# One store ahead of two transposing transfers, two memsets behind a copy: a segment-recurrent attention block with a gated MLP, forward and backward

## The chip, the core and the metric

The kernel runs on one NeuronCore of one Trainium2 chip. A core has TensorE (PE, matrix products into PSUM), VectorE (DVE), ScalarE (ACT), GpSimd (POOL) and SyncE (SP), which here only issues DMA transfers. Each engine works through its own instructions in order and waits on semaphores for the others. The metric is the device time of one execution in microseconds; lower is better. Times of a kernel are the median of several runs. A profile comes from one execution, which has a time of its own.

## The reference

The forward pass, and then the gradients of its result with respect to ten inputs for a given `grad_out`. Inputs are bf16; there are 2048 rows of width 512.

```python
def attention(x, mem):                    # 64 segments of 32 rows, 8 memory rows, 32 heads of 128
    for s in range(64):
        h = concat([mem, x[32*s : 32*s + 32]])           # 40 rows
        q, k, v = h @ Wq, h @ Wk, h @ Wv                 # per head
        p = softmax(where(mask, q @ k.T * 128**-0.5, -1e9))
        o = (p @ v) @ Wo
        mem = o[:8]                                      # goes to the next segment
        yield o[8:]
def mlp(x):                               # hidden width 1792
    return (sigmoid(x @ w_gate) * (x @ w_up)) @ w_down
sa, ca, ga, sb, cb, gb = split(silu(c) @ w_mod, 6)
x = x + ga * attention(layernorm(x) * (1 + ca) + sa, mem0)
x = x + gb * mlp(layernorm(x) * (1 + cb) + sb)
out, vjp = jax.vjp(all_of_the_above);  return out, *vjp(grad_out)
```

The memory rows make the forward pass a recurrence over 64 segments, and the backward pass one in the other direction.

## The kernel before

The kernel has four long stages, one after the other.

- **Forward recurrence** (`phase2`, a loop over s = 0 to 63). A segment projects K, Q and V (`proj`, `v_chunk`), turns them on PE (`turns`), computes the transposed scores and their exponentials (`st_exp`, ACT, into ET), the sums (`den`, `recip`), P V (`pv`), scales it into Ost (`ost`), turns it (`ott_first`, `ott_rest`, into OT), multiplies by Wo (`outproj`) and hands the memory rows on. For the backward pass it stores, by SP, V transposed (VT), P (PS), O (OSR) and O transposed (OT), each a tensor of 128 x 11 x 128 bf16 per segment, and the rows of K and Q (KST, QST).
- **GLU** (`phase3`, the gated MLP, forward and backward, 16 tiles of 128 rows). Its steps s0 to s6 are run as a pipeline, the deepest step first. Behind it come the products for the weight gradients of the MLP, between which the attention weights are loaded and turned.
- **Backward recurrence** (`phase4`, s = 63 to 0).
- **Weight gradients of the attention** (`phase5`).

The order is written out by hand. `pin` ties the instructions of a stretch on one engine to each other in the order of the program; `pin_behind` ties instructions of an engine behind the last one of an earlier stretch. An instruction that is tied by neither goes where its own inputs and buffers let a scheduler put it.

**Around the first edit.** P is made of ET by a transposing SP transfer into Pst (L1065), which the step `norm` (L1157) multiplies on POOL by the reciprocal sums (L1158). Its store to PS is kept in the list `stores_p` (L1161). `norm` of segment s is run in segment s + 1, ahead of the projections (L988), or in segment 63 behind Q's and K's first half there (L1002). The store is issued later in that segment, behind the transposing transfers of V (L1057, into the one buffer VTr) and P (L1065) of the segment itself (L1066). Pst has two buffers, used in turn; the second is `self.Pst1`.

SP's order in segment 62 (NS - 2) is therefore: KST and QST of the segment (L609, L610), L1057, L1065, the store of P of segment 61 ("the last but two"), OSR (L1094), OT (L1133).

In segment 63 the first tile of the GLU is prepared beside the attention (`first_tile_steps`): `add` makes x1 = a * ga + x0 (L770, L771), `stats` (L774 to L777) and `scale` (L780) its normalisation. x1 lies in `first_x1`, which is a view of `self.Pst1`: the buffer of the odd segments, 61 among them. `add` (`first_tile[3]`, L990) stands ahead of K's and Q's projections of segment 63 on DVE, so that DVE's casts of their results (RA1k, RA1q, line L63, in the helper `evac`) come behind it. PE's transposes of RA1k are line L893.

Also in segment 63, POOL issues the loads of the GLU's weights: w_gate and w_up into the place of Wk (L1000, L1001) as soon as K's products are done, w_down into that of Wv (L1044) behind V's. In the GLU, PE reads w_gate from L1341 on, w_up from L1345 on, and w_down in the transposes of L1250.

**Around the second edit.** The last tile's last steps in the GLU: s5 makes hp on PE (L1412); ACT copies it (dh2b, L1418); DVE makes dxh (L1421), pr_cb, junk, bb, cc, ta; ACT tb (L1437); DVE dx (L1439), da, pr_ga; then s6 on PE sums rows into `acc_ps` (L1455) and turns da (L1459). At the end DVE copies `acc_ps` out (L1541, `accs`). Two memsets that belong to the backward recurrence are written further down: of `dOst` (L1602), rows of dO, whose tails are first filled in the third chunk of the last weight gradient of the GLU, and of the first 8 columns of `dyT` (L1861). Nothing ties them, and in the kernel before they stand among the last tile's steps on DVE: the first ahead of dxh, the second between ta and dx.

Of the kernel before, what the change touches and what calls it, by code (L numbers as in the profile page):

```python
# [40 lines left out]
class K:  # L41
# [407 lines left out]
    def phase2(self):  # L449
        nc, tc, cfg, io = self.nc, self.tc, self.cfg, self.io  # L450
        D, DC, H, E, L, M, T, G, NS = cfg.D, cfg.DC, cfg.H, cfg.E, cfg.L, cfg.M, cfg.T, cfg.G, cfg.NS
# [14 lines left out]
        with ExitStack() as ctx:  # L466
# [10 lines left out]
            def ps_f32(name):  # L477
                return psp.tile([128, PG, GW], F32, name=name, tag="p")
# [328 lines left out]
            stores_p = []  # L807
# [34 lines left out]
            def tails_in(xs, s):  # L842
                for x in xs:
                    to_heads("pool", XT[x], btails[s // nseg_t][x][:], 0, 8, 8, 8 * (s % nseg_t))
# [15 lines left out]
            for s in range(NS):  # L860
# [13 lines left out]
                QT, KT, Vst, ET, OT = XT["q"], XT["k"], Vsts[s % 2], ETs[s % 2], OTs[s % 2]  # L874
# [176 lines left out]
                if 0 < s < NS - 1:  # L1051
                    v_chunk(s, 2)
                    v_tails(s + 1)
                    if s4 < 3:
                        tails_in("kq", s + 1)
                if s < NS - 1:
                    nc.sync.dma_start(VTr[:], Vst[:, :], transpose=True)  # L1057
                or2 = ps_f32("or_ps")
                den(0, or2)
# [142 lines left out]
    def phase3(self):  # L1202
# [9 lines left out]
        with ExitStack() as ctx:  # L1212
# [264 lines left out]
            def load_hr(g):  # L1477
                w, n = min(384, F - 384 * g), NT
                (nc.sync if g == 1 else nc.scalar).dma_start(
                    hrs[g][:, 0:n, 0:w], self.HHROWS[0:128 * n, 384 * g:384 * g + w].rearrange("(j p) f -> p j f", p=128))  # L1480
# [12 lines left out]
            def wd_chunk(fc, ps, ot):  # L1493
                if fc >= 3:
                    wd_products(fc, ps, range(NT))
                self.evac("act" if kk[0] % 2 == 0 else "dve", ot[:], ps[:])
                kk[0] += 1
                nc.gpsimd.dma_start(io["out_9"][fc * 128:(fc + 1) * 128, :], ot[:])
# [25 lines left out]
            ET = mybir.EngineType  # L1524
# [14 lines left out]
            self.pin_behind(i0, self.pinned, [ET.PE, ET.DVE, ET.Activation, ET.Pool, ET.SP])  # L1539
            accs = self.flat(self.Wk, 2 * DC * F, 2 * D, F32)  # L1540
            nc.vector.tensor_copy(accs[:], acc_ps[:, :])  # L1541
            for i in range(4):
                nc.gpsimd.dma_start(self.DMOD[2 + i:3 + i, :], accs[32 * i:32 * i + 1, :])

# [3 lines left out]
        with ExitStack() as ctx:  # L1548
            op_ = ctx.enter_context(tc.tile_pool(name="p3g_o", bufs=2, reuse_waits="tile"))
            psG = ctx.enter_context(tc.tile_pool(name="p3g_ps", bufs=4, space=PSUM, reuse_waits="tile"))  # L1550
            setup_pieces = self.p4_weights_setup_pieces(ctx)
            units = 3 * (FC - 3) + 8 * 2 * NCH * DC
            psE = ctx.enter_context(tc.tile_pool(name="p3g_pe", bufs=2, space=PSUM, reuse_waits="tile"))
            n_setup, done = len(setup_pieces), [0]

            def emit_setup(n):
                done[0] += n
                while setup_pieces and (n_setup - len(setup_pieces)) * units < done[0] * n_setup:
                    setup_pieces.pop(0)()
            i0 = len(self.traced())  # L1560
            h2r = self.flat(self.Wk, NT * D, NT * D).rearrange("p (j d) -> p j d", j=NT)
            load_hr(2)
            xrs = []

            def load_xr(i):
                if i < 2 * NCH:
                    rows, ch = ((self.DGROWS, self.DUROWS)[i // NCH], i % NCH)
                    t = ring[i % 2].rearrange("p (j f) -> p j f", j=NT)
                    nc.scalar.dma_start(t, rows[:, ch * CH:(ch + 1) * CH].rearrange("(j p) f -> p j f", p=128))
                    xrs.append(t)  # L1570

            for fc in range(3, FC):
                wd_chunk(fc, psG.tile([128, D], F32, name="gps2", tag="g"), op_.tile([128, D], BF16, name="ot2", tag="o"))
                if fc == 5:
                    load_hr(3)
                elif fc == 8:
                    load_hr(4)
                elif fc == 9:
                    nc.scalar.dma_start(h2r, self.H2ROWS[:, :].rearrange("(j p) d -> p j d", p=128))
                elif fc == 11:  # L1580
                    load_xr(0)
                emit_setup(3)
            load_xr(1)
            k = kk[0]
            for (rows, outw) in ((self.DGROWS, io["out_7"]), (self.DUROWS, io["out_8"])):
                for ch in range(NCH):
                    xr = xrs.pop(0)
                    for c in range(DC):
                        ps = psG.tile([128, CH], F32, name="gps", tag="g")
                        for j in range(NT):  # L1590
                            nc.tensor.matmul(ps[:], lhsT=h2r[:, j, c * 128:(c + 1) * 128], rhs=xr[:, j, :],  # L1591
                                             start=(j == 0), stop=(j == NT - 1))
                        ot = op_.tile([128, CH], BF16, name="ot", tag="o")
                        self.evac("act" if k % 2 == 0 else "dve", ot[:], ps[:])
                        k += 1
                        nc.gpsimd.dma_start(outw[c * 128:(c + 1) * 128, ch * CH:(ch + 1) * CH], ot[:])
                        if c == DC - 1:
                            load_xr(NCH * (outw is io["out_8"]) + ch + 2)
                        emit_setup(8)
                    if outw is io["out_7"] and ch == 0:  # L1600
                        self.get_db(cfg.NS // 4 - 1)
                        nc.vector.memset(self.dOst[:], 0.0)  # L1602
                    if outw is io["out_8"] and ch < 2:
                        self.first_dO_pass(psE, ch)
                    elif outw is io["out_8"] and ch == 2:
                        self.first_dO_turns(psE)
            while setup_pieces:
                setup_pieces.pop(0)()
            self.pin(i0, [mybir.EngineType.SP])
# [37 lines left out]
    def get_da(self, t):  # L1647
        if t not in self.das and t >= 0:
            d = self.dap.tile([128, 4, self.cfg.DC, self.cfg.T], BF16, name="daq")
            self.nc.sync.dma_start(d[:].rearrange("p s c t -> p s (c t)"),  # L1650
                                   self.DAOT[4 * t:4 * t + 4].rearrange("s p c t -> p s (c t)"))
            self.das[t] = d
        return self.das.get(t)
# [60 lines left out]
    def phase4(self):  # L1714
        nc, tc, cfg, io = self.nc, self.tc, self.cfg, self.io
        D, DC, H, E, L, M, T, G, NS = cfg.D, cfg.DC, cfg.H, cfg.E, cfg.L, cfg.M, cfg.T, cfg.G, cfg.NS
# [5 lines left out]
        with self.p4_ctx as ctx:  # L1722
# [52 lines left out]
            def get_dy(s):  # L1775
                if s not in dys:
                    t = dyp.tile([128, DC, 32], BF16, name="dyT")
                    nc.gpsimd.tensor_copy(t[:, :, M:32], get_da(s // 4)[:, s % 4, :, 0:32 - M])
                    dys[s] = t
                return dys[s]  # L1780
# [77 lines left out]
            nc.gpsimd.dma_start(self.DHA[NS, 0:M, :], dSs[0][0:M, 0:D])  # L1858
            self.pin(i0, [mybir.EngineType.Pool, mybir.EngineType.SP])
            dyT = get_dy(NS - 1)  # L1860
            nc.vector.memset(dyT[:, :, 0:M], 0.0)  # L1861
            nseg_t = 128 // T
            row_stores = []

# [664 lines left out]
```

## Time and profile before

| | |
|---|---|
| median of 3 runs | 2963.39 us (2962.72 to 2967.39) |
| the profiled execution, its own time | 2965.28 us |
| its span, first to last instruction | 2963.4 us |
| mean granted clock of PE | 0.998 |
| busy: PE / DVE / ACT / POOL | 98 / 55 / 45 / 42 % of the span |
| forward recurrence, segment 62 to 63 | about 14 us each, to 949 us |
| GLU's pipeline | about 949 to 1275 us |

Reading it: a time in a timeline counts from the start of the span. `[2.32 <-DMA PS<-Pst]` behind a row says that the engine stood idle for 2.32 us ahead of it and what came last of what it waited for. PE's matmuls overlap, so that a busy PE is not a PE at its peak. The granted clock is a share of PE's full clock. Names lose their buffer numbers: `Pst` is either buffer, and `Pst` written by L770 is x1. SPq is SP's DMA queue: a row gives the time of the issue, not that of the transfer. Line L63 is the DVE branch of a helper through which most copies go, L61 the ACT branch.

### The profile page before, as it was taken

How to read it: one execution, taken by the hardware profiler on the slowest of the kernel's cores; microseconds unless marked ns; L12 is line 12 of the kernel's file. 1: busy time of each engine (PE TensorE's matmuls, PEld its weight loads, DVE VectorE, ACT ScalarE, POOL GpSimd, SP SyncE). 2: the span in 40 equal slices, each digit the busy share in tenths (PEclk: the TensorE clock that was granted, in tenths of full speed). 3: DMA queues.
4: the chain of work that ended last, by engine and by line, in shares of the span. 5: the costliest groups of instructions: out<-in, count | busy, mean ns of one | idle time of the engine just before them, and what ended most of it. 6: DMA issues, size and time to landing. Idle time of an engine off the chain costs nothing.

```text
span 2963.4 us, 105252 instructions
## 1 busy us (share of the span) xinstructions
PE 2908.1 (98%) x43764; PEld 1815.4 (61%) x43838; DVE 1630.8 (55%) x3686; ACT 1343.5 (45%) x3245; POOL 1234.7 (42%) x2487
## 2 busy tenths in 40 slices
PE   7999999999998999999999999999999999999999
PEld 3666666666665544445677777777777754445545
DVE  5565666666556888733456666665666642750011
ACT  3666666666666433312355555554555520110011
POOL 2555555555554222221344444444444432762111
PEclk9999999999999999999999999999999999999999
DMA  9888888888889899998699999999999997886565
GB/s 311 230 222 217 227 220 216 222 228 213 217 232 270 216 233 229 242 289 269 189 252 252 253 248 253 258 248 244 253 256 252 250 282 242 255 260 190 164 215 170
DMA packets 838065, 703.00 MB, mean 237 GB/s; under 512 B 537698, under 2 KB 710162, under 8 KB 836692
## 3 DMA queue, kind: packets, MB, share of 16 engines
q1 hardware_dynamic: 711972, 485.29, 65.8%
q0 software_dynamic: 54512, 148.63, 15.5%
q10 hardware_dynamic: 71104, 62.34, 6.6%
q8 instruction: 345, 5.65, 0.8%
q14 instruction: 132, 1.08, 0.1%
HBM read 294.99 MB, written 276.35 MB: 193 GB/s over the span
## 4 chain that ended last, share of the span: by engine, by line
PE 64%; DMA 1%; DVE 1%; issue 1%; ACT 1%; SPq 0%; POOL 0%; DVEq 0%; POOLq 0%; ACTq 0%
PE gps L2308 14%; PE dh_ps L215 8%; PE g_ps L1931 5%; PE pass_ps L257 5%; PE gps5o L2323 4%; PE dhq_ps L223 4%; PE mm L1412 3%; PE gps L1591 3%; PE dh_tps L215 3%; PE mm L1387 2%; PE mm L1372 2%; PE tps L1848 2%; PE mm L1341 1%; PE mm L1345 1%; PE gps L1490 1%; PE turn_ps L1804 1%
## 5 line engine op out<-in xcount | busy, mean ns | idle before, releaser
L2308 PE MATMUL gps<-rows,hrows 128*128 128x512 bf16 (+2 forms) x2124 | 413.6, 355 | 1.9
L2308 PEld LDWEIGHTS <-hrows 128*128 128x128 bf16 x2160 | 211.1, 98 | 204.5 <-issue 0.9
L63 DVE CAST ot<-gps 128x512 bf16<-128x512 f32 (+3 forms) x76 | 48.2, 634 | 307.9 <-PE gps L2308 222.9
L1158 POOL TENSOR_TENSOR Pst<-Pst,rden 120x1408 bf16<-120x1408 bf16 x63 | 159.8, 2537 | 95.6 <-DMA Pst<-ET 95.1
L1976 POOL COPY dOst<-RAd 96x512 bf16<-96x512 bf16 x128 | 75.2, 611 | 296.4 <-DVE RAd L63 296.2
L61 ACT ACTIVATE ot<-gps 128x512 bf16<-128x512 f32 (+3 forms) x75 | 41.2, 549 | 346.4 <-PE gps L2308 242.9
L678 PE MATMUL pass_ps<-Wv,hT 128*32 128x512 bf16 (+2 forms) x2304 | 187.8, 359 | 0.0
L2312 POOL DMA_DIRECT2D out_dram<-ot x104 | 78.6, 756 | 253.7 <-DVE ot L63 130.4
L257 PEld LDWEIGHTS <-hT 128*32 128x32 bf16 x4096 | 114.8, 97 | 99.3 <-issue 7.3
L63 DVE CAST Vst<-pass_ps 96x512 bf16<-96x512 f32 x128 | 87.0, 681 | 106.1 <-ACT RBv L61 97.2
L215 PE MATMUL dh_ps<-WvT,dVT 128*32 128x512 bf16 x2048 | 133.4, 380 | 1.7 <-DVE RBd L63 0.2
L678 PE MATMUL pass_ps<-Wv,hb 128*32 128x512 bf16 (+2 forms) x636 | 126.5, 339 | 0.3 <-POOL hb L430 0.3
L223 PE MATMUL at_ps<-Wo,OT 128*32 128x256 bf16 x4096 | 126.6, 274 | 0.2 <-DVE OT L63 0.2
L257 PE MATMUL pass_ps<-Wk,hT 128*32 128x512 bf16 x2048 | 123.7, 383 | 2.1 <-POOL hT L564 1.1
L223 PE MATMUL dhq_ps<-WqT,dQT 128*32 128x256 bf16 x4096 | 123.2, 273 | 0.2 <-issue 0.2
L257 PE MATMUL pass_ps<-WoT,dyT 128*32 128x256 bf16 (+1 forms) x3072 | 122.4, 308 | 0.9 <-ACT dyT L2057 0.9
L257 PE MATMUL pass_ps<-Wq,hT 128*32 128x512 bf16 x2048 | 122.8, 379 | 0.3 <-DVE RBk L63 0.3
L215 PE MATMUL dh_ps<-WkT,dKT 128*32 128x512 bf16 x2048 | 122.3, 380 | 0.0
L2323 PE MATMUL gps5o<-WoT,rows 128*128 128x512 bf16 x549 | 120.4, 379 | 0.9 <-DMA rows<-OSR 0.4
L850 POOL DMA_DIRECT2D Vst<-RBv x192 | 101.4, 532 | 46.6 <-ACT ET L905 34.2
L223 PEld LDWEIGHTS <-dQT 128*32 128x32 bf16 x4096 | 109.8, 97 | 16.1 <-issue 0.5
L317 DVE TENSOR_TENSOR dST<-dh_ps,dST 128x512 bf16<-128x512 f32 x64 | 44.3, 692 | 129.8 <-ACT dST L316 129.8
(481 smaller groups left out, 7050.3 us busy)
## 6 DMA issues: line engine op xcount, KB each, us to landing
OSR<-Ost SPq DMA_DIRECT2D x64, 352.0 KB
OT<-OT SPq DMA_DIRECT2D x64, 352.0 KB
Pst_l<-PS SPq DMA_DIRECT2D x64, 352.0 KB
OT_l<-OT SPq DMA_DIRECT2D x64, 352.0 KB
DVR<-rows_x POOLq DMA_DIRECT2D x64, 352.0 KB, 6.4
DKR<-rows_x POOLq DMA_DIRECT2D x64, 352.0 KB, 5.8
DQR<-rows_x POOLq DMA_DIRECT2D x64, 352.0 KB, 3.1
VT<-VTr SPq DMA_DIRECT2D x63, 352.0 KB
```

The lines of the kernel that those rows point to most:

```text
L63: return nc.vector.tensor_copy(out, in_)
L215: self.nc.tensor.matmul(ps[32 * j:32 * j + 32, :], lhsT=lhsT, rhs=w, start=(n < 4), stop=(n >= total - 4), tile_position=(0, 32 * j))
L223: nc.tensor.matmul(ps[32 * j:32 * j + 32, :], lhsT=x[k], rhs=w[k][:, 256 * d:256 * d + 256], start=(n == 0), stop=(n == total - 1), tile_p ...
L257: self.nc.tensor.matmul(ps[32 * j:32 * j + 32, :], lhsT=lhs(c), rhs=rhs, start=(c == 0), stop=(c == DC - 1), tile_position=(0, 32 * j))
L678: nc.tensor.matmul(ps[32 * j:32 * j + 32, o * E:(o + n) * E], lhsT=lhsT, rhs=wc[:, 3 * a + hl:3 * (a + n - 1) + hl + 1:3, :], start=(c == ...
L850: nc.gpsimd.dma_start(Vst[96 + 8 * j:104 + 8 * j, :], rb[32 * j + o:32 * j + o + 8, :])
L1158: nc.gpsimd.tensor_tensor(Pst[0:120, :, :], Pst[0:120, :, :], rden[:, :].unsqueeze(2).to_broadcast([120, G, 128]), op=ALU.mult)
L1412: nc.tensor.matmul(hp[:], lhsT=xT[:, fc, :], rhs=wT[:, fc, :], start=(n == 0), stop=(n == 2 * FC - 1))
L1591: nc.tensor.matmul(ps[:], lhsT=h2r[:, j, c * 128:(c + 1) * 128], rhs=xr[:, j, :], start=(j == 0), stop=(j == NT - 1))
L1931: nc.tensor.matmul(ps[:, j, 0:w], lhsT=lh[:, g * GW:(g + 1) * GW], rhs=rh[:, g * GW:g * GW + w], start=True, stop=True)
L2308: nc.tensor.matmul(ps[:, 0:ng * E], lhsT=hrows[:, tp_, c * 128:(c + 1) * 128], rhs=rows[:, tp_, 0:ng * E], start=(tp_ == 0), stop=(tp_ == ...
L2323: nc.tensor.matmul(pss[gg][:], lhsT=rows[:, t, gg * E:(gg + 1) * E], rhs=dyrows[:, t, :], start=(n == 0), stop=(n == NTP - 1))
```

## The change

The store of P of segment 61 is issued in segment 62 ahead of the transposing transfers of V and P instead of behind them; it waits for the same POOL multiplication. On SP this is one transfer that moves past two. The two memsets are tied behind the GLU's last copy on DVE (`accs`, L1541); on DVE they then stand right behind it, in the order dOst, dyT. No other instruction changes its place on any engine.

```diff
                 if s < NS - 1:
+                    if s == NS - 2:
+                        stores_p.pop()()
                     nc.sync.dma_start(VTr[:], Vst[:, :], transpose=True)
...
             nc.vector.tensor_copy(accs[:], acc_ps[:, :])
+            behind = self.accs_copied = {ET.DVE: self.traced()[-1]}
...
                         self.get_db(cfg.NS // 4 - 1)
+                        i1 = len(self.traced())
                         nc.vector.memset(self.dOst[:], 0.0)
+                        self.pin_behind(i1, behind, [ET.DVE])
...
             dyT = get_dy(NS - 1)
+            i1 = len(self.traced())
             nc.vector.memset(dyT[:, :, 0:M], 0.0)
+            self.pin_behind(i1, self.accs_copied, [mybir.EngineType.DVE])
```

## The prediction, made before the changed kernel was run

> **What bounds the kernel now.** I read the page first, then TensorE's waits, then the timelines around the two edited places.
>
> ```profile
> span 2963.4 us, 105252 instructions
> PE 2908.1 (98%) x43764; PEld 1815.4 (61%) x43838; DVE 1630.8 (55%) x3686; ACT 1343.5 (45%) x3245; POOL 1234.7 (42%) x2487
> ```
>
> TensorE (PE) is busy for 2908.1 of 2963.4 us: 55.3 us of idle time in all. A change that moves no matmul can only win some of that, or of time in which PE runs at a lower clock. So the question is what idle time the two edits touch. The first edit sits in segment 62 of the forward recurrence (step s = NS - 2), and the waits of PE behind it have one large entry:
>
> ```profile
> PE turn_ps L893 <- DVE RA1k L63: 3.3, 1, 3.3
> ```
>
> It is one wait of 3.3 us, in segment 63. The timelines of PE, VectorE (DVE) and GpSimd (POOL) show how it comes about; their columns are start, duration, engine, line, what:
>
> ```profile
> 933.93 0.62 PE L893 MATMUL turn_ps<-ident,RA1k 128*128 128x128 bf16 x8 [3.33 <-DVE RA1k L63]
> ...
> 926.00 0.46 DVE L337 CAST at_tb<-at_ft 128x128 bf16<-128x128 f32 x1 [0.59 <-ACT hT L1139]
> 928.77 3.78 DVE L770 TENSOR_TENSOR Pst<-RBk,sa_bc 128x512 f32<-128x512 bf16 x1 [2.32 <-DMA PS<-Pst]
> 932.58 0.69 DVE L771 TENSOR_TENSOR Pst<-Pst,RBk 128x512 f32<-128x512 f32 x1
> 933.19 0.68 DVE L63 CAST RA1k<-pass_ps 128x512 bf16<-128x512 f32 x1
> ...
> 913.78 2.53 POOL L1158 TENSOR_TENSOR Pst<-Pst,rden 120x1408 bf16<-120x1408 bf16 x1 [3.38 <-DMA Pst<-ET]
> 929.44 2.55 POOL L1158 TENSOR_TENSOR Pst<-Pst,rden 120x1408 bf16<-120x1408 bf16 x1
> ```
>
> DVE is free at 926.46, but L770 writes x1 into the buffer from which P of segment 61 is still being stored, and waits 2.32 us for that store. It then runs 3.78 us, where its neighbour L771, of the same 128x512 with two SBUF inputs, takes 0.69. The extra 3.09 us lie under the POOL multiplication of 929.44 to 931.99. So the late store costs twice: the wait, and starting into that multiplication. Whether it is the overlap that stretches it, this trace shows only by these rows; without it I take 0.69. Behind L770 stands RA1k (933.19 instead of about 927.8), and behind RA1k stands PE.
>
> The idle time has a second price. The windows view (length, busy times with counts, then granted PE clock, DMA share, GB/s) of the idle stretch and the two after it:
>
> ```profile
> 930.60:933.93 3.33, 0.01 (x2) 0.00 (x1) 3.29 (x4) 0.00 (x0) 1.39 (x1) 1.00 0.84 293
> 933.93:938.17 4.24, 4.24 (x42) 2.27 (x43) 4.06 (x11) 1.21 (x4) 0.57 (x1) 0.65 1.02 387
> 938.17:939.40 1.23, 1.23 (x20) 1.21 (x21) 0.06 (x1) 1.18 (x4) 1.15 (x2) 0.81 1.09 400
> ```
>
> After the idle time the granted clock is 0.65 for 4.24 us and 0.81 for 1.23 us: 4.24 x 0.35 + 1.23 x 0.19 = 1.48 + 0.23 = 1.72 us of PE time lost. What stands to be won here is 3.33 + 1.72 = **5.05 us**.
>
> **The change, part one: the store.** One SP transfer, the store of P of segment 61, moves ahead of the two transposing transfers of segment 62. Nothing is added or removed. SP's queue and its waits there:
>
> ```profile
> 918.63 0.42 SPq L610 DMA_DIRECT2D QST<-RA0q  x1
> 920.86 1.28 SPq L1057 DMA_TRANSPOSE VTr<-Vst  x1
> 924.06 1.61 SPq L1161 DMA_DIRECT2D PS<-Pst  x1
> ...
> SPq L1057 <- DMA VT<-VTr: 1.5, 1, 1.5
> ```
>
> The store's own condition, the POOL multiplication, is met at 913.78 + 2.53 = 916.31. SP is free at 919.05 and stands until 920.86, since the first transposing transfer waits for its buffer VTr (1.5 us of it) and then for the last V columns. The store drops into that gap: 1.81 us, where its issue took 1.61 even when crowded. So the transposing transfers are issued no later, and the store starts some 5 us earlier (919.1 for 924.06). Do they then move their data later? The DMA share (last column but one) of the same microseconds:
>
> ```profile
> 920.00:921.00 1.00, 1.00 (x24) 0.94 (x22) 0.43 (x2) 0.96 (x5) 0.53 (x3) 1.00 0.44 153
> 921.00:922.00 1.00, 0.62 (x10) 0.39 (x7) 0.97 (x3) 1.00 (x4) 0.00 (x0) 1.00 0.04 13
> PS<-Pst SPq DMA_DIRECT2D x3, 352.0 KB
> ```
>
> From 920 to 922 the engines are busy 0.44 and 0.04 of the time: 0.56 + 0.96 = 1.52 us are free, room for 0.59 MB at the 387 GB/s of the stretch above. The store has 352 KB, 0.36 MB, 0.93 us: it fits into that hole. When does it land? Below: 919.1 + 0.9, so 920.0. Above: in the old order its landing freed L770 at 928.77, 4.71 us after its issue, behind two transposes; the same 4.71 from 919.1 gives 923.8. Both lie ahead of 926.46, where DVE asks. Then L770 and L771 run at 0.69 each, done by 927.9 (926.46 + 1.38), 1.5 us before the POOL multiplication at 929.44; RA1k follows by 928.6, and PE, which comes for it at 930.60, doesn't wait. The whole 5.05 us are gone at 939.40, where the clock was back.
>
> What is late next? Segment 63 leads into the GLU, whose weights are loaded meanwhile:
>
> ```profile
> 928.66 0.76 POOL L1001 DMA_DIRECT2D Wk<-in_B_w_up_dram  x1
> 938.80 1.17 POOL L1044 DMA_DIRECT2D Wv<-in_B_w_down_dram  x1
> ...
> Wk<-in_B_w_up_dram POOLq DMA_DIRECT2D x1, 1792.0 KB, 16.4
> Wv<-in_B_w_down_dram POOLq DMA_DIRECT2D x1, 1792.0 KB, 13.0
> ...
> 949.62 0.92 PE L1345 MATMUL mm<-Wk,Wq 128*128 128x448 bf16 x4
> 954.92 0.94 PE L1250 MATMUL tp<-ident,Wv 128*128 128x128 bf16 x14
> ```
>
> w_up lands at 928.66 + 16.4 = 945.1, w_down at 938.80 + 13.0 = 951.8. PE, 5.05 us earlier, wants them at 944.57 and 949.87: both would be late, by 0.5 and 1.9 us. The load of w_down is issued earlier as well, but w_up is then still under way in the same queue, and the DMA engines are full (share 1.02 and 1.09 above). What helps them is that the 0.36 MB of the store have gone through the hole before, 0.93 us of transfer. I take w_down at 951.8 - 0.93 = 950.9, and w_up at 944.1, in time. PE waits at L1250 from 949.9 to 950.9, and the gain that is left is 954.92 - 950.9 = **4.0 us**. Bounds: 3.1 if the loads don't move, 5.05 if w_down follows its earlier issue.
>
> **Part two: the two memsets.** They move behind the copy L1541 on DVE. Timelines of DVE and ScalarE (ACT) at the end of the GLU:
>
> ```profile
> 1256.52 0.69 DVE L1421 SCALAR_TENSOR_TENSOR dxh<-mm,Wv 128x512 f32<-128x512 f32 x1 [6.35 <-ACT dh2b L1418]
> 1269.19 0.65 DVE L1602 MEMSET dOst<- 128x704 uint32 x1 [5.94 <-PE mm L1412]
> 1269.75 0.64 DVE L1421 SCALAR_TENSOR_TENSOR dxh<-mm,Wv 128x512 f32<-128x512 f32 x1
> 1272.47 0.07 DVE L1861 MEMSET dyT<- 128x16 uint32 x1
> 1272.74 0.69 DVE L1439 TENSOR_TENSOR dx<-ta,tb 128x512 f32<-128x512 f32 x1 [0.20 <-ACT tb L1437]
> 1275.28 0.68 DVE L1541 COPY Wk<-acc_ps 128x512 f32<-128x512 f32 x1
> 1278.81 0.69 DVE L63 CAST ot<-gps 128x512 bf16<-128x512 f32 x1 [2.85 <-PE gps L1490]
> ...
> 1255.89 0.60 ACT L1418 ACTIVATE dh2b<-mm 128x512 bf16<-128x512 f32 x1 [5.51 <-remote]
> 1269.07 0.60 ACT L1418 ACTIVATE dh2b<-mm 128x512 bf16<-128x512 f32 x1 [5.51 <-PE mm L1412]
> ```
>
> This chain does hold PE up. But dxh waits for ACT's dh2b anyway: a tile earlier dh2b ended at 1256.49 and dxh began at 1256.52. In the last tile dh2b ends at 1269.67; without the memset dxh starts at 1269.70 instead of 1269.75. The 0.65 us lay under dh2b, and their removal is worth **0.05 us**; the small one lay in the wait for tb, and is worth 0. At the new place both (0.72 us) fall into 2.85 us in which DVE waits for PE; if that cover were gone, they would cost 0.72. Bounds of part two: 0 and 1269.75 - 1269.19 = 0.56 us gained.
>
> Sum: 4.0 + 0.05 = 4.05 us. The profiled execution took 2965.28 us (span 2963.4), 1.89 above the median of the three runs, 2963.39. So 2961.2 against its own time, **2959.3 us** against the median; a gain of 0.14%, below 0.2% (5.9 us), about what a measurement of this kernel can tell from no change.
>
> **The rivals.**
> A, all is won: w_down comes earlier with its issue, and PE never waits. For it: that issue stands behind DVE and PE work that moves by 5 us. Against it: the queue was already continuous. 5.05 + 0.05 = 5.1: 2958.3.
> B, the GLU start is set by DMA, and only the 0.93 us of the earlier bytes stay: 2962.4. For it: the chain of waits runs through a store here for 10.88 us. Against it: PE doesn't stand in that stretch (4.89 of 5 us busy):
>
> ```profile
> 943.23 10.88 DMA OT<-OT
> 955.00:960.00 5.00, 4.89 (x79) 4.44 (x78) 3.56 (x7) 4.88 (x7) 0.86 (x2) 1.00 0.75 213
> ```
>
> C, slower: the wait at L1250 takes the place of the old one, with its clock loss. Segment 63's stores of V, O and the transposed O (three of P's 352 KB, 1.08 MB) are issued 5 us earlier and compete with w_down. If they take their whole 1.08 MB / 387 GB/s = 2.8 us from it, it lands at 950.9 + 2.8 = 953.7; PE stands for 3.8 us, longer than the 3.33 that brought the clock down, and pays 1.72 again: 953.7 + 1.72 = 955.4 against 954.92, 0.5 us slower, 2963.9. It decides from a landing at 953.2. [...] Against C:
>
> ```profile
> 933.33 0.39 SPq L1161 DMA_DIRECT2D PS<-Pst  x1
> 943.67 5.07 SPq L1198 DMA_DIRECT2D Wv<-AOA  x4
> SPq L1198 <- DMA PS<-Pst: 2.0, 1, 2.0
> ```
>
> The store issued at 933.33 is still waited for after 943.67. SP's queue has a backlog of ten microseconds, so stores that join it earlier stand behind it and take nothing more from w_down.
> D, the store isn't early: SP would stand at it for a POOL result or a free slot, and the transposes behind it. The 916.31 above speaks against that; 2963.3.
>
> **How the numbers follow.** Forecast 0.55, A 0.22, B 0.12, C 0.06, D 0.05. The likeliest alone, with its bounds of 3.1 and 4.6, spans 2958.7 to 2960.3. The range goes from A with the upper bound of part two (2957.8), less the 0.7 us by which the fastest run lies under the median, to C: 2957.1 to 2963.9. Faster by over 0.2% (below 2957.5) needs A at its upper end: 0.10. Slower by over 0.2% needs C with a far later landing: 0.03. Within: 0.87.
>
> **What would show it.** Right: the store's issue at about 919 on SP ahead of L1057's transfer; L770 at about 926.5 for 0.69 us; no idle time at L893; the clock at 1.00 from 930 to 940; a wait of PE for w_down of about 1 us at L1250's place; dxh 0.03 us behind dh2b, the memsets behind L1541. Wrong: L770 still over 1 us long or waiting; a wait for w_down over 2 us; DVE's dxh starting before dh2b has ended; or L1158 of segment 62 pushed past 930.5 by a later transposed P.

## The result and the profile after

The changed kernel takes **2960.55 us** (median of 21 runs, 2958.37 to 2963.97); the kernel before, run beside it, 2964.38 us (21 runs, 2961.34 to 2967.41). The ratio is 0.9987, with a 95% interval of 0.9981 to 0.9992: 3.83 us less. The prediction was 2959.3 us, 4.05 us less.

The page of the changed kernel; its profiled execution took 2959.51 us. In the changed kernel the lines of the file stand 2 further down behind L1057, and up to 7 further down behind L1861.

```profile
span 2957.7 us, 105328 instructions
PE 2910.6 (98%) x43838; PEld 1814.5 (61%) x43838; DVE 1627.7 (55%) x3686; ACT 1344.2 (45%) x3245; POOL 1239.0 (42%) x2487
```

The busy times are those of before to within 0.4%, as they should be for a change that moves no work. Spans of single executions differ for other reasons too (see the last section), so the timelines are the better measure. I count each instruction from the same point in each kernel, the start of K's products of segment 63, which stands ahead of all that the store can reach. The rows of it, first of before, then of the changed kernel:

```profile
926.11 1.91 PE L257 MATMUL pass_ps<-Wk,hT 128*32 128x512 bf16 x32 [0.38 <-ACT hT L1139]
```

```profile
925.87 1.91 PE L257 MATMUL pass_ps<-Wk,hT 128*32 128x512 bf16 x32 [0.38 <-ACT hT L1141]
```

So 0.24 us of any difference between these two profiles was there before the change acts. Now the first edit. SP, DVE, PE and POOL of the changed kernel, start and duration in us:

```profile
918.36 0.45 SPq L1163 DMA_DIRECT2D PS<-Pst  x1
920.62 1.40 SPq L1059 DMA_TRANSPOSE VTr<-Vst  x1
...
926.00 0.71 DVE L770 TENSOR_TENSOR Pst<-RBk,sa_bc 128x512 f32<-128x512 bf16 x1
926.75 0.77 DVE L771 TENSOR_TENSOR Pst<-Pst,RBk 128x512 f32<-128x512 f32 x1
927.45 0.68 DVE L63 CAST RA1k<-pass_ps 128x512 bf16<-128x512 f32 x1
...
930.29 0.62 PE L893 MATMUL turn_ps<-ident,RA1k 128*128 128x128 bf16 x8
...
929.20 2.55 POOL L1160 TENSOR_TENSOR Pst<-Pst,rden 120x1408 bf16<-120x1408 bf16 x1
934.26 1.17 POOL L1044 DMA_DIRECT2D Wv<-in_B_w_down_dram  x1
```

The store sits in SP's gap, L1059 follows at 920.62 (0.24 earlier than L1057 in before, which is the offset: no later, no earlier). L770 has no wait and takes 0.71 us for 3.78, PE comes to L893 with no idle time. The clock in two of the stretches that the prediction shows for before (PEclk is the number behind POOL's):

```profile
930.60:933.93 3.33, 3.33 (x57) 2.44 (x54) 2.56 (x8) 2.11 (x8) 1.90 (x3) 1.00 0.94 372
933.93:938.17 4.24, 3.78 (x84) 3.01 (x85) 3.94 (x11) 3.23 (x10) 2.16 (x4) 1.00 1.03 377
```

1.00 in both, where before had 0.65 in the second. How much of it is kept? DVE's t (L1274, L1276 in the changed kernel) comes once per tile and serves as a milestone. Its first three in before and in the changed kernel:

```profile
948.80 0.69 DVE L1274 TENSOR_TENSOR t<-Wk,Wv 128x512 f32<-128x512 bf16 x1
964.64 0.69 DVE L1274 TENSOR_TENSOR t<-Wv 128x512 f32<-128x512 bf16 x1
982.21 0.69 DVE L1274 TENSOR_TENSOR t<-Wv 128x512 f32<-128x512 bf16 x1
```

```profile
943.50 0.69 DVE L1276 TENSOR_TENSOR t<-Wk,Wv 128x512 f32<-128x512 bf16 x1
959.63 0.68 DVE L1276 TENSOR_TENSOR t<-Wv 128x512 f32<-128x512 bf16 x1
978.15 0.68 DVE L1276 TENSOR_TENSOR t<-Wv 128x512 f32<-128x512 bf16 x1
```

948.80 - 943.50 - 0.24 = **5.06** us: all that was to be won. Then 964.64 - 959.63 - 0.24 = **4.77**, and 982.21 - 978.15 - 0.24 = **3.82**. Between the first and the second t 0.29 us are lost, between the second and the third 0.95; the twelve t that follow stand at 3.82 to 3.83. At these two places stand two waits of PE, of which the prediction had the first alone (in brackets, the idle time ahead of the row and what ended it):

```profile
949.94 0.95 PE L1252 MATMUL tp<-ident,Wv 128*128 128x128 bf16 x14 [0.16 <-DMA Wv<-in_B_w_down_dram]
966.61 0.60 PE L1389 MATMUL mm<-Wv,hhT 128*128 128x512 bf16 x2 [1.74 <-DMA hhT<-hh]
```

hhT is hh, turned by a transposing transfer of SP. DVE has hh done at about 955.05, and SP issues the transfer at 960.85, behind loads of x, attention output and grad_out for later tiles. In before it was 961.24. Counted from K's products that is 34.98 for 35.13, only 0.15 us earlier, while PE came 4.77 us earlier:

```profile
961.24 3.39 SPq L1365 DMA_TRANSPOSE hhT<-hh  x1
```

```profile
953.96 1.09 DVE L1351 TENSOR_TENSOR hh<-sg,u 128x1792 bf16<-128x1792 bf16 x1
...
956.58 3.05 SPq L1200 DMA_DIRECT2D Wv<-AOA  x4
...
960.85 3.43 SPq L1367 DMA_TRANSPOSE hhT<-hh  x1
```

The second edit, on ACT and DVE of the changed kernel:

```profile
1264.99 0.60 ACT L1420 ACTIVATE dh2b<-mm 128x512 bf16<-128x512 f32 x1 [5.51 <-PE mm L1414]
1265.62 0.69 DVE L1423 SCALAR_TENSOR_TENSOR dxh<-mm,Wv 128x512 f32<-128x512 f32 x1 [6.45 <-ACT dh2b L1420]
1266.24 0.08 DVE L1423 DVE_READ_ACCUMULATOR dxh<-mm,Wv 128x1 f32 x1
1268.66 0.69 DVE L1441 TENSOR_TENSOR dx<-ta,tb 128x512 f32<-128x512 f32 x1 [0.22 <-ACT tb L1439]
1271.20 0.68 DVE L1543 COPY Wk<-acc_ps 128x512 f32<-128x512 f32 x1
1271.98 0.65 DVE L1606 MEMSET dOst<- 128x704 uint32 x1
1272.58 0.07 DVE L1867 MEMSET dyT<- 128x16 uint32 x1
1274.73 0.69 DVE L63 CAST ot<-gps 128x512 bf16<-128x512 f32 x1 [2.09 <-PE gps L1492]
```

ACT's dh2b ends at 1264.99 + 0.60 = 1265.59, and dxh now starts 0.03 us behind it, as forecast. But dx stands 1272.74 - 1268.66 - 0.24 = 3.84 us ahead of before, and the lead was 3.83 at the last t already: the edit is worth about 0.01, not 0.05.

### The profile page after: what moved, and what is told of

The parts are those of the page before. It is cut to its first block, busy times and chain, and to the rows that moved or that the text cites. A ratio compares the mean times of both kernels' runs of the same rounds, so it can differ in the third digit from the quotient of the medians.

```text
span 2957.7 us, 105328 instructions
## 1 busy us (share of the span) xinstructions
PE 2910.6 (98%) x43838; PEld 1814.5 (61%) x43838; DVE 1627.7 (55%) x3686; ACT 1344.2 (45%) x3245; POOL 1239.0 (42%) x2487
## 4 chain that ended last, share of the span: by engine, by line
PE 63%; issue 2%; DMA 1%; DVE 1%; ACT 1%; POOL 0%; DVEq 0%; SPq 0%; POOLq 0%; ACTq 0%
PE gps L2315 14%; PE dh_ps L215 8%; PE g_ps L1938 5%; PE pass_ps L257 5%; PE gps5o L2330 4%; PE dhq_ps L223 4%; PE mm L1414 3%; PE dh_tps L215 3%; PE gps L1594 2%; PE mm L1389 2%; PE mm L1374 2%; PE tps L1853 2%; PE mm L1343 1%; PE mm L1347 1%; PE gps L1492 1%
## 5 line engine op out<-in xcount | busy, mean ns | idle before, releaser
L63 DVE CAST ot<-gps 128x512 bf16<-128x512 f32 (+3 forms) x76 | 48.2, 634 | 306.8 <-PE gps L2315 222.7
L63 DVE CAST Vst<-pass_ps 96x512 bf16<-96x512 f32 x128 | 87.3, 682 | 106.2 <-ACT RBv L61 94.1
```

Of the source, the lines that this page charges most:

```text
L63: return nc.vector.tensor_copy(out, in_)
```

## The experiments

The shift is the lead over before in us, counted from K's products of segment 63: at the first, second and third t, and at the first ot behind the GLU (L63, 1278.81 in before). The waits are those of PE, in us; 0 is no row of that wait (one under 0.15 us has none). Each ratio is to runs of before that were made beside it, with its 95% interval.

| kernel | wait L893 | wait w_down | wait hhT | 1st t | 2nd t | 3rd t | ot | median us, ratio |
|---|---|---|---|---|---|---|---|---|
| changed | 0 | 0.16 | 1.74 | 5.06 | 4.77 | 3.82 | 3.84 | 2960.55, 0.9987 (0.9981 to 0.9992) |
| e1, store only | 0 | 0.43 | 1.89 | 5.05 | 4.49 | 3.40 | 3.42 | 2960.75, 0.9993 (0.9984 to 1.0002) |
| e2, memsets only | 2.60 | 0 | 0 | 0.60 | 0.60 | 0.60 | -1.06 | 2963.59, 1.0 (0.9991 to 1.0008) |
| e3, POOL later | 0 | 0 | 1.82 | 4.27 | 4.27 | 3.24 | 3.26 | 2961.03, 0.9991 (0.9982 to 1.0) |
| e4, store between | 0 | 0.71 | 2.02 | 5.06 | 4.21 | 2.99 | 3.00 | 2962.03, 0.9994 (0.9986 to 1.0003) |
| e5, w_down later | 0 | 1.25 | 0.33 | 4.25 | 2.87 | 2.87 | 2.89 | 2961.04, 0.9992 (0.9983 to 1.0001) |
| e6, hhT first | 0 | 0 | 0 | 5.06 | 5.06 | 5.05 | 5.06 | 2960.36, 0.9991 (0.9983 to 1.0) |
| e7, hhT first in before | 3.33 | 0 | 0 | 0.33 | 0.33 | 0.32 | -1.30 | 2962.83, 0.9997 (0.9988 to 1.0006) |
| e8, changed again | 0 | 0 | 1.55 | 5.06 | 5.05 | 4.29 | 4.30 | 2962.53, 0.9987 (0.9978 to 0.9996) |
| e9, e6 again | 0 | 0 | 0 | 5.06 | 4.88 | 4.88 | 4.90 | 2961.30, 0.9983 (0.9974 to 0.9992) |
| e10, e6 without the memsets' tie | 0 | 0 | 0 | 5.06 | 5.01 | 5.01 | 3.34 | 2960.64, 0.9986 (0.9977 to 0.9995) |

The intervals of the times are some 2.6 us to either side: they can't tell the kernels with an early store from each other. The shifts can, to a few hundredths up to the first t and to some 0.5 us behind it: changed and e8, and e6 and e9, are the same kernels.

**e1 and e2: each part alone.** e1 has only the first edit of the diff, e2 only the ties of the memsets.

> The kernel before with the store of P of segment 61 moved ahead of the two transposing transfers, and nothing else. My theory: all but 0.05 us of the changed kernel's gain is the store's. L770 starts at about 926.0 to 926.5 and runs about 0.7 us, PE has no idle time at L893, the granted clock stays at 1.00 from 930 to 940; the shift of the instructions of the GLU against the kernel before is 5.0 to 5.3 us at its first tile and 4.0 to 4.1 from its fourth tile on; time about 2960.5 (ratio 0.9987). Rival: the memsets bring a good part of it; then this kernel gains clearly less, 2 us or under.

> The kernel before with the two memsets tied behind the copy of the accumulators (L1541), and the store where it was. My theory: L770 still waits about 2.3 us and takes about 3.8 us, PE idles 3.3 us at L893; the last dxh of the GLU comes 0.03 to 0.05 us behind dh2b and the sum is 0.05 us, a ratio of 1.000. Rival: up to 0.56 us gained, if what dxh waits for is the memset and not dh2b.

e1 does at L770, L893 and the clock what the changed kernel does. Its shift from the third t on, 3.40 to 3.42, is below the 4.0 to 4.1 that I expected and 0.4 below the changed kernel's; e8, which is the changed kernel again, lies 0.5 above. These differences arise at the waits for w_down and hhT, ahead of the memsets: scatter of two DMA landings. e2 keeps PE's wait at L893 (2.60 us) and the clock loss. By the timelines the gain is the store's; by its time alone e1 can't be told from before (the interval reaches 1.0002).

e2 showed more than it was built for, and not what I expected of L770. It reached segment 63 1.35 us earlier by its own clock, and there the partners had changed. DVE and POOL of e2:

```profile
927.00 0.69 DVE L770 TENSOR_TENSOR Pst<-RBk,sa_bc 128x512 f32<-128x512 bf16 x1 [1.90 <-DMA PS<-Pst]
927.73 3.47 DVE L771 TENSOR_TENSOR Pst<-Pst,RBk 128x512 f32<-128x512 f32 x1
...
928.09 2.55 POOL L1158 TENSOR_TENSOR Pst<-Pst,rden 120x1408 bf16<-120x1408 bf16 x1
```

(1.35 is 926.11 less the start of K's products in e2, 924.76.) Here L770 waited for the store, but had ended before POOL's multiplication began: 0.69 us. Now it is L771 that lies beside it, and it takes 3.47 us in place of 0.69. So the stretch belongs to neither instruction; it goes to the one that meets L1158. Both end 0.56 us behind it (932.55 against 931.99 in before, 931.20 against 930.64 here).

**e3: the late store stays, POOL's multiplication goes.**

```diff
                     nc.gpsimd.dma_start(self.w_up, io["B_w_up"].rearrange("(c p) f -> p c f", p=128))
-                    norms.pop()()
...
                 if s == NS - 1:
                     first_tile[4]()
+                    norms.pop()()
```

> The kernel before with its late store, but GpSimd's multiplication of segment 62 (L1158) moved from ahead of x1's two DVE operations (L770, L771) to behind the tokens' part of segment 63, so that it no longer runs beside them. My theory, contention with that multiplication: L770 still waits about 2.3 us for the store and starts at about 928.8, but takes about 0.7 us; RA1k is done by about 930.8, PE idles 0.3 us or less at L893 and keeps its clock at 1.00; most of the 4 us is gained, 3 to 4 us, without touching the store. Rival: L770 is stretched by the store or by what else lies on the buffer, and still takes 2 us or more; then PE idles as before and nothing is gained.

```profile
927.90 0.69 DVE L770 TENSOR_TENSOR Pst<-RBk,sa_bc 128x512 f32<-128x512 bf16 x1 [1.77 <-DMA PS<-Pst]
928.63 0.69 DVE L771 TENSOR_TENSOR Pst<-Pst,RBk 128x512 f32<-128x512 f32 x1
...
930.23 0.62 PE L893 MATMUL turn_ps<-ident,RA1k 128*128 128x128 bf16 x8
...
932.17 2.53 POOL L1158 TENSOR_TENSOR Pst<-Pst,rden 120x1408 bf16<-120x1408 bf16 x1
```

L770 still waits 1.77 us for the store, and nothing follows from it: both run 0.69 us, PE doesn't stand, the clock stays. In before L770 began 0.56 us later behind K's products (2.66 for 2.10). In e3 RA1k is done 2.02 us behind L770's start (929.92 less 927.90); by that it would have been done at 928.77 + 2.02 = 930.79 in before, and PE came for it at 930.60. So in before **the wait for the store alone would have cost PE some 0.2 us (an estimate); it was dear because it pushed x1 under POOL's multiplication.** The multiplication at its new place costs 0.79 us (4.27 for 5.06): among others, or_ps then waits 0.6 us for DVE. What the two engines share there, no run shows. The rows show that the DVE operation beside L1158 took 3.78 us (before) and 3.47 (e2) against 0.69 away from it, while L1158 took 2.55 in both. Nor do the recorded starts (those of POOL are rough) tell which of the two is held up: L770 stands 0.67 us ahead of L1158 in before, L771 0.36 ahead in e2, and both lost. In the changed kernel it went the other way: L770 starts at 926.00 and keeps its 0.71 us, and POOL's copy of ao_tail, which starts at 926.01, takes 0.97 us, where it took 0.41 in before.

**e4: the store between the two transposing transfers.**

```diff
                     nc.sync.dma_start(VTr[:], Vst[:, :], transpose=True)
...
                 if s < NS - 1:
                     Pst = Psts[s % 2]
+                    if s == NS - 2:
+                        stores_p.pop()()
                     nc.sync.dma_start(Pst[:], ET[:, :], transpose=True)
```

> The kernel before with the store put between the two transposing transfers instead of ahead of both: it misses the gap of SP before 920.86, and most of the hole in which the DMA engines are idle. Issue at about 922.2. If what counts is only that the store has landed when L770 asks for its buffer (926.0 to 926.5): with the 4.7 us from issue to landing of the kernel before it lands at about 926.9, L770 waits 0 to 0.5 us, runs 0.7 us, PE does not idle at L893, and the gain there is the full 5 us; the transposed P comes up to 1.6 us later, and with it POOL's multiplication L1158. If the hole matters as the prediction took it (0.93 us of transfer), w_down lands about 0.9 us later than in the changed kernel and PE waits about 1 us at tp; gain 3 us. Rival: the gap ahead of both transfers is what the gain hangs on; then L770 waits 2 us or more.

```profile
922.82 0.83 SPq L1163 DMA_DIRECT2D PS<-Pst  x1
...
927.28 0.69 DVE L770 TENSOR_TENSOR Pst<-RBk,sa_bc 128x512 f32<-128x512 bf16 x1 [0.25 <-POOL ao_tail L2389]
```

The first t stands at 5.06 as well: SP's gap isn't needed. x1 may come later than in the changed kernel, too: L770 starts 0.59 us behind K's products here (927.28 less 926.69), 0.13 there (926.00 less 925.87), and even e3's 2.10 (927.90 less 925.80) doesn't make PE stand at L893. What follows is 0.83 us worse than in the changed kernel (2.99 for 3.82), with the longest wait for hhT of all and, e5 apart, the longest for w_down. That fits a store that takes its 0.93 us of transfer (the prediction's estimate) later, but e8 and the changed kernel, which are the same, lie 0.47 apart: suggested, not shown.

**e5: w_down issued later.**

```diff
                     first_tile[5]()
-                    nc.gpsimd.dma_start(self.w_down, io["B_w_down"].rearrange("(fc p) d -> p fc d", p=128))
...
                 self.pop_later()
                 if s == NS - 1:
+                    nc.gpsimd.dma_start(self.w_down, io["B_w_down"].rearrange("(fc p) d -> p fc d", p=128))
```

> The changed kernel with the load of w_down issued by POOL some 3 us later, behind the two deferred writes of segment 63's attention (about 937.5 for 934.26). In the changed kernel it lands 1.94 us earlier than before (949.86 for 951.8), twice what the prediction took, and PE waits 0.16 us for it. Theory bandwidth, the prediction's: the queue is continuous, w_down follows w_up, its landing is set by the bytes ahead of it and its issue does not matter; it still lands at 950 to 950.5 and PE waits 0.2 to 0.7 us, as in the two runs with the early store; time within 0.5 us of the changed kernel's. Rival, the prediction's rival A: it came earlier because it was issued earlier; then it lands at about 953, PE waits 3 us or more at tp and the gain is 1 us or less.

The timeline of e5 (PE, POOL, SP), then the DMA issues of e5 and of the changed kernel (last number: us from issue to landing):

```profile
925.38 1.91 PE L257 MATMUL pass_ps<-Wk,hT 128*32 128x512 bf16 x32 [0.38 <-ACT hT L1141]
937.63 1.11 POOL L1093 DMA_DIRECT2D Wv<-in_B_w_down_dram  x1
951.35 0.95 PE L1252 MATMUL tp<-ident,Wv 128*128 128x128 bf16 x14 [1.25 <-DMA Wv<-in_B_w_down_dram]
959.09 3.01 SPq L1367 DMA_TRANSPOSE hhT<-hh  x1
966.61 0.61 PE L1389 MATMUL mm<-Wv,hhT 128*128 128x512 bf16 x2 [0.33 <-DMA hhT<-hh]
```

```profile
Wv<-in_B_w_down_dram POOLq DMA_DIRECT2D x1, 1792.0 KB, 13.7
```

```profile
Wv<-in_B_w_down_dram POOLq DMA_DIRECT2D x1, 1792.0 KB, 15.6
```

Counted from K's products, the issue comes at 12.25 and the landing at 12.25 + 13.7 = 25.95 us. In the changed kernel it was 8.39 + 15.6 = 23.99; in before, with the late store, 12.69 + 13.0 = 25.69. So with an early store and a late issue w_down lands about where it did in before. e3 says the same from the other side: there the store is late, the issue comes at 935.68 - 925.80 = 9.88, and PE takes w_down at 950.34 - 925.80 = 24.54 without a wait. **My theory falls: it is the issue and not the store's bytes.** The rival is half right: 3.86 us of issue are worth 1.96 us of landing, not 3.86, by one execution of each.

PE's wait for hhT falls from 1.74 to 0.33, but not because hhT is there earlier. SP issues it 1.27 us earlier (33.71 for 34.98), and PE still starts on it at 966.61 - 925.38 = 41.23, where the changed kernel did at 966.61 - 925.87 = 40.74. It is PE that comes 1.90 us later (the lead at the second t is 2.87 for 4.77). So these runs do not show that w_down, issued earlier, holds up hhT. POOL's issue at its new place also holds up ao_tail, for which PE waits 0.6 us; that is most of the 0.81 that is missing at the first t already (4.25 for 5.06). Behind both waits the shift is 2.87, 0.95 worse.

**e6, e7: hhT ahead of tile 3's loads.** On SP, the loads of tile 3 and later are tied behind hhT of tile 0; e6 is the changed kernel with the tie, e7 the kernel before with it.

```diff
             def load(j):
...
+                i1 = len(self.traced())
                 ins[j] = self.glu_first.get(j) or self.glu_load(j, nc.sync)
+                if "hhT" in last:
+                    self.pin_behind(i1, last["hhT"], [ET.SP])
...
                 nc.sync.dma_start(hhT[:], st["hh"][:], transpose=True)
+                if j == 0:
+                    last["hhT"] = {ET.SP: self.traced()[-1]}
```

> The changed kernel with SP's loads of the GLU's tile 3 and later tied behind the transposing transfer hhT of tile 0. In the changed kernel, and in each of the three runs in which PE does not stand at L893, PE waits 1.7 to 2.0 us for hhT, and 0.95 to 1.22 us of the gain go there; hh is done at about 955.3 but hhT is issued at 960.85, behind prefetches in SP's queue. Theory: the wait is SP's order; with hhT ahead of tile 3's loads it is issued 2 us or more earlier, PE's wait for hhT is gone or under 0.5 us, and the shift against the kernel before stays at 4.5 to 4.8 us through the GLU where it was 3.8 (less, if the wait of 1.0 us for DVE's Wq of the kernel before comes back); time 0.5 to 1 us below the changed kernel's. Rival: hhT is late because the transposing transfer itself is slow beside the other transfers; then the wait stays at 1 us or more and nothing is gained.

> The kernel before with the same tie of tile 3's loads behind hhT, store and memsets as before. Theory: the wait for hhT is what comes next when the first one goes; in the kernel before PE gets to hhT's product 5 us later and does not wait for it, so the tie brings nothing (shift 0.0 to 0.2 us through the GLU). Rival: hhT holds up the GLU in both kernels, then this one gains about 1 us as well.

e6, SP and PE:

```profile
926.87 1.91 PE L257 MATMUL pass_ps<-Wk,hT 128*32 128x512 bf16 x32 [0.38 <-ACT hT L1141]
957.40 2.16 SPq L1371 DMA_TRANSPOSE hhT<-hh  x1
966.83 0.61 PE L1241 MATMUL tp<-ident,Wk 128*128 128x128 bf16 x8 [0.81 <-DVE Wq L63]
```

hhT is issued at 957.40 - 926.87 = 30.53, where it was 34.98: 4.45 us earlier. PE no longer waits for it, and the shift stays at 5.05 to 5.06 at every t and behind the GLU, more than the 4.5 to 4.8 expected. The 0.81 us for DVE's Wq are a wait that before has too (1.02 there, behind one matmul fewer), and they are why a wait of 1.74 us for hhT costs only 0.95: in each of the five profiles with that wait above 1 us the loss is the wait less 0.8 (1.74 and 0.95, 1.89 and 1.09, 1.82 and 1.03, 2.02 and 1.22, 1.55 and 0.76). In e7 the lead is 0.33 us at the first t already, ahead of hhT, and no more by the third: without the store there is nothing to be won at hhT. The wait is what becomes late next, not a cost of its own.

**e8 to e10: the tie with and without the memsets, beside the changed kernel.** e8 is the changed kernel, e9 is e6, e10 is e6 with the memsets where they were.

> The changed kernel once more, beside the two below. Expected from the shift of its timeline: 3.8 us below the kernel before, ratio 0.9987.

> The changed kernel with tile 3's loads behind hhT once more. Its timeline stood 5.06 us ahead of the kernel before at every tile of the GLU, the whole of the idle time and the clock loss, 1.2 us more than the changed kernel's 3.83. Theory: the time follows, ratio 0.9983, 1.2 us below the changed kernel in the same call. Rival: the 1.2 us are given back after the GLU; then both have the same time.

> The kernel before with the early store and the tie of tile 3's loads behind hhT, the memsets where they were. Theory: the memsets' new place is worth nothing, since dxh that begins 0.06 us earlier after a wait also takes 0.05 us longer; the shift is 5.0 to 5.1 us at every tile and behind the GLU as well, and the time is that of the kernel above. Rival: the memsets were worth 0.05 us or more; then the shift behind the GLU is 4.95 us or less.

The ratios to before are 0.9987, 0.9983 and 0.9986, and the medians 2962.53, 2961.30 and 2960.64. e9 and e10 are below e8, by 1.2 and 1.9 us, but the intervals overlap: that the times follow the shift fits and isn't shown. In the timelines the lead at the third t is 4.29, 4.88 and 5.01 (expected: 3.8, 5.06 and 5.0 to 5.1). From the last t to ot e10's shift falls from 5.02 to 3.34, 1.68 us, e2's from 0.62 to -1.06, 1.68, and e7's from 0.34 to -1.30, 1.64; the last section says what that is. The memsets show in none of the three.

## Why the prediction was right, and where it was not

- **5.05 us to be won at L893, 3.33 of idle time and 1.72 of clock**: right. 5.05 or 5.06 at the first t in seven of the eight profiles with an early store (e5 has a new wait ahead of it), and the clock at 1.00.
- **L770's 3.78 us are the overlap with POOL's multiplication**: right; taken there from a few rows, and shown by e2 (the stretch goes over to L771) and e3 (it goes with L1158). That the late store "costs twice" is not right: the wait by itself was worth some 0.2 us (an estimate, by e3).
- **The store drops into SP's gap and the hole of the DMA engines; the transposing transfers are not held up**: right, 918.36 and 920.62. Neither was necessary for the 5.06 (e4).
- **w_down is late next, PE waits 1.0 us for it, net 4.0**: the step that failed. It lands at 934.26 + 15.6 = 949.86; counted from K's products that is 23.99 for 25.69 in before, 1.70 us earlier and not 0.93, and PE waits 0.16. I had it come forward by the bytes of the store; e5 and e3 show that it comes forward by its own issue, by about half. That is rival A's mechanism at half its size.
- **What is late next was not asked once more behind w_down**: hhT is missing from the sum. It takes 0.95 us, nearly what w_down was to take. That the sum of 4.05 is so close to the shift of 3.8 is luck: one cost that I put in at 1.05 us (5.05 less 4.0) was 0.29, and one of 0.95 that I left out was there.
- **Rival C**, the stores taking from w_down: not seen; w_down came earlier. The backlog of SP that I quoted against C is what made hhT late: with part of it moved behind hhT, PE doesn't wait for hhT (e6, e9, e10).
- **Rivals B and D**: B's landing didn't hold (PE has only the waits above); D is excluded by 918.36.
- **The memsets, 0.05**: the row was read right (dxh starts 0.03 us behind dh2b), the end was not. In before dxh started straight behind the memset, took 0.64 us and reached its accumulator read 0.56 us after its start (1269.75, 1270.31); in the changed kernel it started after 6.45 us of idle time, took 0.69 and reached it after 0.62 (1265.62, 1266.24). The 0.06 us of earlier start are spent on it. Worth 0.01 or less; no cost at the new place, as forecast.

## What to carry to other kernels

A wait that costs next to nothing in itself can be dear for what it pushes its engine into (here some 0.2 us by itself, an estimate, and 5.05 us with POOL's multiplication beside L770): look at what the instruction runs beside once it has waited, and try taking that away too. Once a stall is gone, walk on along the critical engine until the shift is constant: there was a second late input 17 us behind the first, a transfer at the end of a queue of prefetches. Where the time can't resolve an edit, count both traces from a common instruction ahead of it and read the lead at milestones.

## What the runs showed of the hardware

**The clock loss came in pieces of one size.** Wherever the granted clock fell in the twelve profiles of this case, it went to 0.50 and cost 1.70 to 1.72 us (its length times the share of the clock that was missing), so some 3.4 us at one half (an estimate: 1.71 / 0.50): after an idle time of 3.33 us in before (the prediction's rows) and after 2.60 in e2 the same:

```profile
931.86:933.86 2.00, 2.00 (x22) 1.35 (x25) 1.93 (x5) 1.21 (x4) 0.37 (x1) 0.70 1.03 400
933.86:935.86 2.00, 2.00 (x22) 0.99 (x15) 1.60 (x7) 0.00 (x0) 0.20 (x1) 0.50 1.04 374
935.86:937.86 2.00, 1.82 (x28) 1.19 (x23) 1.11 (x4) 1.48 (x5) 1.33 (x2) 0.94 1.02 394
```

2.00 x 0.30 + 2.00 x 0.50 + 1.82 x 0.06 = 1.71. Whether it falls isn't settled by the length of the idle time: 2.02 us (e4, hhT) left it at 1.00, while after the 1.8 us in which PE waits for da behind the GLU, in every profile, it fell in e2, e7 and e10 and not in the other nine. Two microseconds of e2, and then before, behind that wait:

```profile
1274.00:1275.00 1.00, 1.00 (x4) 0.38 (x3) 0.67 (x2) 0.00 (x0) 1.00 (x3) 0.51 0.96 145
1275.00:1276.00 1.00, 1.00 (x4) 0.38 (x3) 0.00 (x0) 0.00 (x0) 1.00 (x3) 0.50 0.96 303
```

```profile
1274.21:1276.21 2.00, 1.80 (x13) 0.92 (x14) 1.75 (x3) 1.09 (x2) 1.27 (x3) 1.00 0.66 205
```

That is the 1.7 us by which the shifts of these three fall at ot, and part of the scatter between executions: a profile had none to four such stretches (before three, the changed kernel two, the same kernel as e8 none). It is not all of it: the slowest profiled execution, e1's with 2968.50 us, had two. What settles whether the clock goes down, no run here shows: it went down after idle times of 3.33 us (before), 2.60 (e2) and 1.8 (e2, e7, e10), and stayed at 1.00 after 2.02 (e4).
